# Computing the last group's slot shares ahead of the first expert layer

## The chip, the cores and the metric

The kernel runs on one core of a Trainium2 chip. The metric is the time of one execution on the device, in microseconds (us). All arithmetic is float32. TensorE (PE in the profile) multiplies and transposes; its weight loads are listed apart as PEld. VectorE (DVE), ScalarE (ACT) and GpSimd (POOL) do the element-wise work, and SyncE (SP) issues nearly all transfers between main memory and the core.

## The reference

Two blocks run one after the other. The first is a causal attention with exponential decay, without softmax, worked in blocks of the sequence with a carried state; its output is the input x (3072 rows of 512) of the second, a mixture of experts with soft routing: 8 experts of 4 slots each.

```python
logits = x @ phi                                  # 3072 x 32
d = exp(logits - logits.max(0)); d /= d.sum(0) + 1e-9     # over the rows, for each slot
slot_input = (d.T @ x).reshape(8, 4, 512)
for e in range(8):
    h = maximum(slot_input[e] @ w1[e], 0)         # 512 -> 1024, first layer
    slot_out[e] = h @ w2[e]                       # 1024 -> 512, second layer
c = exp(logits - logits.max(1)); c /= c.sum(1) + 1e-9     # over the slots, for each row
y = c @ slot_out
```

The shares c are needed only in the last line. They depend on the logits alone, so that they can be computed anywhere between the logits and the output.

## The kernel before, in words

The 3072 rows are cut into 24 tiles of 128 rows, two of which make a unit of the attention loop (line 483), and four make a group of the routing. For each of the six groups, `logits` (line 362) computes the logits with the slots on the partitions, keeps a running maximum and sum for d, and leaves a raw copy in `L`; `slot_softmax` (line 406) computes that group's shares c from the logits turned to rows on the partitions (`lp`), and writes them to `CN`. It is a generator with three stops: DVE takes a maximum (`cmx`) and subtracts it (`ce`), ACT takes the exponential; DVE sums (`cs`), adds 1e-9 and inverts; POOL multiplies into `CN`. Inside the loop a group's shares are computed in the unit after its logits. The last group has no unit after it, so its `lp` is made behind the loop: PE turns `L` into the PSUM bank `tr` (line 615).

Then come the experts. Their 4 + 4 split makes two units, Q = 0 and Q = 1. `first(Q, between)` (line 656) multiplies the slot inputs with w1 into two PSUM banks, one for each half of the 1024 hidden columns: `gl` and `xb` for Q = 0, `xa` and `tr` for Q = 1. So the second unit of the first layer writes over the bank in which `lp` lies. Its matmuls go in four steps of 128 input columns (kc), and in each step first to one bank (four matmuls), then to the other. After them ACT (bank 0) and DVE (bank 1) apply the scale and the ReLU into `h`, and DVE turns `h` in two pieces into `hz`, the weights of the second layer. In the first unit, `denominators` (line 644) runs between kc = 1 and kc = 2: it makes the second half of the slot inputs (`e`, turned by DVE, which kc = 2 and 3 read) and the scale `rown`.

`second(part, dst, fill)` (line 694) is the second layer. It makes the output's columns in two halves: `kv` for the first, `xa` for the second. In each half the blocks of Q = 0 come before those of Q = 1. During the second half the outputs of the first are already made (`spread`, `put`), and those of the second half follow at the end. The last group's `CN` is first read in `last_C` (line 768), during the second half.

Every engine works its instructions in the order in which this program text issues them (`InOrder`, line 38), and each waits where it reads or overwrites what another engine has not finished. The instructions below line 713 are therefore in this order on each engine.

Weights of w1 lie in 32 buffers of the pool `slabs`, all loaded long before the first layer. As the first unit gives these buffers back, the 16 remaining pairs of w2 tiles (`w2p`, 512 KB each) are loaded into them by the loop of line 714, and later `h`, `hz`, the spread sums and the outputs `o` take buffers of the same pool, in the order in which buffers become free.

Of the kernel before, what the change touches and what calls it, by code (L numbers as in the profile page):

```python
# [23 lines left out]
G = T // 4  # L24
# [29 lines left out]
def decay_attn_soft_moe(  # L54
# [23 lines left out]
    def bank(tag):  # L78
        return ps.tile([P, 512], F32, tag=tag, name=tag)
# [35 lines left out]
    def load_two(pool_=slabs, tag="slab", bufs=None):  # L115

        (Q, f, q), _ = late.pop(), late.pop()
        t_ = pool_.tile([P, 2, 512], F32, tag=tag, name="w2p", bufs=bufs)
        sp.dma_start(out=t_, in_=w2[4 * Q + q:4 * Q + q + 2, f].rearrange("e p d -> p e d"))
        for i in range(2):  # L120
            wt["w2", Q, q + i, f] = t_[:, i, :]
# [39 lines left out]
    for hh in range(2):  # L161
        for hp in range(HP):
            x = hh * HP + hp
# [242 lines left out]
    def slot_softmax(g, lp):  # L406

        lv = lp.rearrange("p (g s) -> p g s", g=4)
        cmx = small.tile([P, 4], F32, tag="cmx", name="cmx")
        dve.tensor_reduce(out=cmx, in_=lv, axis=AX.X, op=ALU.max)  # L410
        ce = small.tile([P, 4, SL], F32, tag="ce", name="ce", bufs=1)
        dve.tensor_tensor(
            out=ce, in0=lv, in1=cmx.rearrange("p (g o) -> p g o", o=1).broadcast_to([P, 4, SL]), op=ALU.subtract
        )
        act.activation(out=ce, in_=ce, func=AF.Exp)
        cs = small.tile([P, 4], F32, tag="cs", name="cs")
        yield
        dve.tensor_reduce(out=cs, in_=ce, axis=AX.X, op=ALU.add)
        dve.tensor_scalar(out=cs, in0=cs, scalar1=1e-9, scalar2=None, op0=ALU.add)
        dve.reciprocal(out=cs, in_=cs)  # L420
        yield
        pool.tensor_tensor(
            out=CN[:, 4 * g:4 * g + 4, :],
            in0=ce,
            in1=cs.rearrange("p (g o) -> p g o", o=1).broadcast_to([P, 4, SL]),
            op=ALU.mult,
        )
        yield
# [185 lines left out]
    lp = bank("tr")[:, 0:P]  # L614
# [41 lines left out]
    def first(Q, between=None):  # L656
        ph = [bank("gl"), bank("xb")] if Q == 0 else [bank("xa"), bank("tr")]
        for kc in range(4):
            for nf in range(2):
                for q in range(4):  # L660
                    pe.matmul(
                        out=ph[nf][SL * q:SL * q + SL, :],
                        lhsT=sT[:, kc, :],
                        rhs=wt["w1", Q, q, kc][:, nf, :],
                        start=(kc == 0),
                        stop=(kc == 3),
                    )
            if between is not None and kc == 1:
                between()
        if Q == 1:  # L670
            hz.append(slabs.tile([P, 32, SL], F32, tag="slab", name="hz"))
        h = slabs.tile([P, 2, 512], F32, tag="slab", name="h")
        act.activation(out=h[:, 0], in_=ph[0], func=AF.Relu, scale=rown[:, Q:Q + 1])
        dve.tensor_scalar(out=h[:, 1], in0=ph[1], scalar1=rown[:, Q:Q + 1], scalar2=0.0, op0=ALU.mult, op1=ALU.max)

        for nf in range(2):
            dve.transpose(
                out=hz[Q][:, 16 * nf:16 * nf + 16].rearrange("p a b -> p (a b)"), in_=h[:, nf]
            )
# [3 lines left out]
    def quad(dst, Q, f, w, start, stop):  # L683
        for q in range(4):
            pe.matmul(
                out=dst[SL * q:SL * q + SL],
                lhsT=hz[Q][:, 4 * f + q],
                rhs=w(q),
                start=start,
                stop=stop,  # L690
                skip_group_check=True,
            )

    def second(part, dst, fill):
# [13 lines left out]
        for n, (d_, Q, f, w) in enumerate(todo):  # L708
            if n in fill:
                fill[n]()  # L710
            quad(d_, Q, f, w, n == 0, n == len(todo) - 1)

    first(0, denominators)
    while late:
        load_two()
    for x in slot_softmax(G - 1, lp):
        pass
    first(1)

    so = work.tile([P, D], F32, tag="at", name="so", bufs=4)  # L720
# [119 lines left out]
```

## Time and profile before

| | us |
|---|---|
| median of 3 runs | 162.25 (162.06 to 162.30) |
| the profiled execution | 162.07 |
| its span, from the first to the last instruction | 160.3 |
| PE busy in it | 145.9 |
| DVE, ACT, POOL busy | 81.3, 49.4, 48.4 |

The span is 1.77 us shorter than the time of the same execution: what lies before the first and behind the last instruction. In the rows below, one matmul of the program is up to two records, since a float32 product is recorded in parts: a row with x8 is four matmuls of the first layer. Every instruction of the program carries line 48, where a helper issues it, so that rows are told apart by the names of the tiles. Names are printed without buffer numbers (`sc` is `sc0` or `sc1`, `s` is `s4`).

### The profile page before, as it was taken

To read this page: it belongs to the slowest core of one execution; us is meant where nothing else is said; L and a number is where in the kernel's file an instruction comes from. 1 tells how busy PE (TensorE), PEld (TensorE's weight loads), DVE (VectorE), ACT (ScalarE), POOL (GpSimd) and SP (SyncE) were. 2 spreads that over 40 slices of the span, in tenths; PEclk is the share of its full clock that TensorE was granted. 3 is DMA by queue.
4 is the path that set the end of the run, shared out by engine and by line. 5 is a ranking of instruction groups with operands and counts; after the bars stand their busy time and mean duration, and the time that the engine had idled before them with its cause. 6 is when DMAs were issued, how large, how long until landed. Compare 5 with 4: busy or idle time off the path is not lost.

```text
span 160.3 us, 5707 instructions
## 1 busy us (share of the span) xinstructions
PE 145.9 (91%) x2403; PEld 111.3 (69%) x2403; DVE 81.3 (51%) x184; ACT 49.4 (31%) x113; POOL 48.4 (30%) x63
## 2 busy tenths in 40 slices
PE   7899999999999999999999999999959999996900
PEld 7779998789879997998979897874212464652600
DVE  1996447383767287727754755543151311622720
ACT  3112433334431445061516151442010101621610
POOL 1288923642923083732282552000000000000000
PEclk9999999999999999999999999999999999999975
DMA  5999999999999999999999996999999999799497
GB/s 166 328 394 400 413 405 408 408 408 412 410 406 411 410 415 404 414 400 385 404 407 404 404 327 189 354 360 374 405 404 408 408 404 403 271 315 335 152 384 255
DMA packets 30745, 59.16 MB, mean 369 GB/s; under 512 B 2944, under 2 KB 9216, under 8 KB 30720
## 3 DMA queue, kind: packets, MB, share of 16 engines
q1 hardware_dynamic: 30576, 58.80, 97.0%
q8 instruction: 19, 0.31, 0.8%
q14 instruction: 6, 0.05, 0.1%
q10 hardware_dynamic: 144, 0.01, 0.1%
HBM read 52.50 MB, written 6.29 MB: 367 GB/s over the span
## 4 chain that ended last, share of the span: by engine, by line
PE 85%; DVE 5%; DMA 2%; ACT 1%; issue 1%; DVEq 1%
PE xa L48 20%; PE sc L48 17%; PE tr L48 12%; PE gl L48 12%; PE kv L48 10%; PE xb L48 10%; PE dp L48 3%; DMA lam_sb<-lam_x 2%; DVE mask L48 2%; DVE qpow L48 1%; DVE hz L48 1%; ACT o L48 1%; DVEq L836 1%; DVE h L48 0%; DVE so L48 0%
## 5 line engine op out<-in xcount | busy, mean ns | idle before, releaser
L48 POOL TENSOR_TENSOR qs<-ld,qpow 128x512 f32<-128x512 f32 x20 | 25.3, 1276 | 11.0 <-PE xb L48 6.0
L48 ACT COPY x<-sc 128x512 f32<-128x512 f32 x22 | 11.8, 589 | 33.5 <-PE sc L48 33.5
L48 DVE TENSOR_TENSOR at<-sc,mask 128x512 f32<-128x512 f32 x24 | 15.4, 684 | 9.1 <-PE sc L48 9.1
L48 POOL TENSOR_TENSOR dec<-st,qpow 128x256 f32<-128x256 f32 x16 | 9.9, 621 | 26.8 <-DVE st L48 26.8
L48 PEld LDWEIGHTS sc<-ld 64*128 64x128 f32 x192 | 11.6, 187 | 5.5 <-issue 5.4
L48 PE MATMUL sc<-ld 64*128 64x128 f32 x192 | 13.9, 285 | 0.0
L48 PE MATMUL tr<-ld 64*128 64x128 f32 x96 | 12.7, 273 | 0.7 <-DMA ld<-kT 0.7
L48 DVE TENSOR_TENSOR st<-dec,kv 128x256 f32<-128x256 f32 x16 | 6.6, 413 | 13.1 <-PE kv L48 12.9
L48 PE MATMUL xa<-at,ld 128*64 128x128 f32 x192 | 13.1, 279 | 0.0
L48 PE MATMUL dp<-ld 64*128 64x128 f32 x96 | 12.7, 273 | 0.0
L48 PE MATMUL xb<-at,ld 128*64 128x128 f32 x192 | 12.5, 273 | 0.0
L48 PEld LDWEIGHTS tr<-ld 64*128 64x128 f32 x96 | 11.6, 188 | 0.9 <-DMA ld<-qT 0.9
L48 PE MATMUL sc<-ident,xt 128*128 128x128 f32 x88 | 12.0, 280 | 0.0
L48 PEld LDWEIGHTS dp<-ld 64*128 64x128 f32 x96 | 11.6, 188 | 0.0
L48 PEld LDWEIGHTS xa<-at,ld 128*64 128x64 f32 x192 | 10.2, 136 | 2.0 <-issue 1.8
L48 PE MATMUL xa<-qs,st 64*64 64x128 f32 x160 | 11.4, 277 | 0.0
L48 PE MATMUL xb<-qs,st 64*64 64x128 f32 x160 | 11.4, 277 | 0.0
L48 POOL TENSOR_TENSOR vd<-ld,mask 128x512 f32<-128x512 f32 x9 | 9.6, 1061 | 5.1 <-DVE mask L48 5.1
L48 PEld LDWEIGHTS sc<-ident,xt 128*128 128x128 f32 x88 | 9.4, 141 | 1.9 <-issue 1.4
L48 PEld LDWEIGHTS xb<-at,ld 128*64 128x64 f32 x192 | 10.6, 137 | 0.0
L48 DVE TENSOR_TENSOR kn<-dp,mask 128x512 f32<-128x512 f32 x10 | 6.9, 691 | 6.8 <-PE dp L48 6.8
L48 PEld LDWEIGHTS xa<-qs,st 64*64 64x64 f32 x160 | 8.5, 132 | 1.5 <-issue 0.2
(162 smaller groups left out, 283.2 us busy)
## 6 DMA issues: line engine op xcount, KB each, us to landing
slab<-w_x SPq DMA_DIRECT2D x32, 512.0 KB, 7.0
w2p<-w_x SPq DMA_DIRECT2D x18, 512.0 KB, 9.9
w2t<-w_x SPq DMA_DIRECT2D x28, 256.0 KB, 5.5
ld<-kT SPq DMA_DIRECT2D x24, 256.0 KB, 6.9
ld<-qT SPq DMA_DIRECT2D x24, 256.0 KB, 6.6
ld<-vN SPq DMA_DIRECT2D x24, 256.0 KB, 6.9
y<-o SPq DMA_DIRECT2D x24, 256.0 KB, 3.5
L<-phi_x SPq DMA_DIRECT2D x1, 64.0 KB, 4.4
```

The source lines that it names most:

```text
L48: return self._tc.keep_in_program_order(f(*args, **kwargs))
L836: with tile.TileContext(nc) as tc:
```

## The change

The two lines that run the last group's `slot_softmax` stand ahead of `first(0, denominators)` in place of behind it and behind the loads of w2. Nothing else is edited.

```diff
+    for x in slot_softmax(G - 1, lp):
+        pass
     first(0, denominators)
     while late:
         load_two()
-    for x in slot_softmax(G - 1, lp):
-        pass
     first(1)
```

On DVE, before, from the product `wl` (the last instruction ahead of the first layer) to the inverse of the sum `cs`; `e`, `rden` and `rown` belong to `denominators`, `h` and `hz` to the end of the first unit:

```order
L48 TENSOR_TENSOR wl<-wgt,lsum 128x1
L48 STREAM_TRANSPOSE e<-dp 128x32 x2
L48 TENSOR_SCALAR rden<-sc_2097 128x1
L48 RECIPROCAL rden<-rden 128x1
L48 TENSOR_TENSOR rown<-own_125,rden 128x2
L48 TENSOR_SCALAR h<-xb,rown 128x512
L48 STREAM_TRANSPOSE hz<-h 128x512 x2
L48 TENSOR_REDUCE cmx<-tr 128x4
L48 TENSOR_TENSOR ce<-tr,cmx 128x128
L48 TENSOR_REDUCE cs<-ce 128x4
L48 TENSOR_SCALAR cs<-cs 128x4
L48 RECIPROCAL cs<-cs 128x4
```

And in the changed kernel, from the same product to the same transposes:

```order
L48 TENSOR_TENSOR wl<-wgt,lsum 128x1
L48 TENSOR_REDUCE cmx<-tr 128x4
L48 TENSOR_TENSOR ce<-tr,cmx 128x128
L48 TENSOR_REDUCE cs<-ce 128x4
L48 TENSOR_SCALAR cs<-cs 128x4
L48 RECIPROCAL cs<-cs 128x4
L48 STREAM_TRANSPOSE e<-dp 128x32 x2
L48 TENSOR_SCALAR rden<-sc_2107 128x1
L48 RECIPROCAL rden<-rden 128x1
L48 TENSOR_TENSOR rown<-own_125,rden 128x2
L48 TENSOR_SCALAR h<-xb,rown 128x512
L48 STREAM_TRANSPOSE hz<-h 128x512 x2
```

Five instructions have gone ahead of seven others. On ACT the exponential of `ce` stands ahead of the first unit's `h` in the same way; POOL's order is unchanged.

On PE the order is unchanged, but not what is waited for. These are the first matmuls of `first(1)`, with the semaphores that they wait for in brackets; lines with - are of before, with + of the change:

```order
 L48 MATMUL xa<-slab,e 32x512 [waits Activation_49]
 L48 MATMUL xa<-slab,e 32x512 x3
-L48 MATMUL tr<-slab,e 32x512 [waits DVE_49]
-L48 MATMUL tr<-slab,e 32x512 x3
+L48 MATMUL tr<-slab,e 32x512 x4
 L48 MATMUL xa<-slab,e 32x512 x3
```

The first matmul into `tr` no longer carries a wait of its own for DVE.

On SP the order is unchanged too, but buffers of the pool are given out in another order. These are the last loads of w2 and the first output:

```order
 L48 DMA w2p<-w_x 128x2x512 [waits DMAHW5_49,PE_49]
 L48 DMA w2p<-w_x 128x2x512 [waits DMAHW6_49,PE_49]
-L48 DMA w2p<-w_x 128x2x512 [waits DMAHW7_49,DVE_49,Activation_49]
+L48 DMA w2p<-w_x 128x2x512 [waits DMAHW7_49,PE_49]
 L48 DMA y<-o 128x2x256 [waits DMAHW0_49,Activation_49]
```

The sixteenth load went into the buffer of the first unit's `h`; now it goes into that of the first w1 tile of the second unit, and `h`, `hz` and the first spread sum behind it each take the next buffer.

## Rows read from the trace of the kernel before

**Rows 1.** The page: busy time, share of the span and instructions of each engine

```profile
PE 145.9 (91%) x2403; PEld 111.3 (69%) x2403; DVE 81.3 (51%) x184; ACT 49.4 (31%) x113; POOL 48.4 (30%) x63
```

**Rows 2.** The page: the queue of SP's transfers: packets, MB, share of 16 engines

```profile
q1 hardware_dynamic: 30576, 58.80, 97.0%
```

**Rows 3.** The page: the chain that ended last, by engine

```profile
PE 85%; DVE 5%; DMA 2%; ACT 1%; issue 1%; DVEq 1%
```

**Rows 4.** That chain in order of time: start us, us, what

```profile
117.83 0.75 DVE h L48
118.58 1.21 DVE hz L48 x2
119.79 0.19 DVE cmx L48
...
120.07 0.30 DVE ce L48
120.37 0.04 issue
120.41 1.06 PE tr L48 x8
...
126.63 6.95 PE kv L48 x128
```

**Rows 5.** Timeline of PE, first layer: start, us, what [idle before, releaser]

```profile
116.64 1.04 PE L48 MATMUL xb<-slab,e 128*32 128x512 f32 x8
117.50 1.04 PE L48 MATMUL xa<-slab,e 128*32 128x512 f32 x8
120.41 1.06 PE L48 MATMUL tr<-slab,e 128*32 128x512 f32 x8 [1.88 <-DVE ce L48]
121.30 1.04 PE L48 MATMUL xa<-slab,e 128*32 128x512 f32 x8
```

**Rows 6.** Timeline of DVE over the same stage

```profile
110.07 0.16 DVE L48 TENSOR_TENSOR wl<-wgt,lsum 128x1 f32<-128x1 f32 x1
113.77 0.31 DVE L48 STREAM_TRANSPOSE e<-dp 128x32 f32<-128x32 f32 x2 [3.54 <-PE sc L48]
...
119.71 0.25 DVE L48 TENSOR_REDUCE cmx<-tr 128x4 f32<-128x128 f32 x1
...
121.26 0.18 DVE L48 RECIPROCAL cs<-cs 128x4 f32<-128x4 f32 x1
...
127.36 1.29 DVE L48 STREAM_TRANSPOSE hz<-h 128x512 f32<-128x512 f32 x2
```

**Rows 7.** Timeline of ACT over the same stage

```profile
108.48 0.59 ACT L48 COPY CN<-xa 128x512 f32<-128x512 f32 x1
116.89 0.69 ACT L48 ACTIVATE h<-gl,rown 128x512 f32<-128x512 f32 x1 [7.83 <-PE gl L48]
120.39 0.31 ACT L48 ACTIVATE ce<-ce 128x128 f32<-128x128 f32 x1 [2.81 <-DVE ce L48]
```

**Rows 8.** Tile w2p: loads and use; ns min/median/max, first and last start us

```profile
L48 PE MATMUL xa<-w2p,hz x128: 379/379/404, 133.4 to 145.6; 128*32 128x256 f32 x128
L48 SPq DMA_DIRECT2D w2p<-w_x x18: 367/384/822, 108.3 to 128.5; - x18
...
DMA to landing us min/median/max: 6.0/9.9/10.8
```

**Rows 9.** Stretches: us, busy of PE, PEld, DVE, ACT, POOL, PEclk, DMA share, GB/s

```profile
144.00:148.00 4.00, 2.58 (x45) 1.07 (x37) 1.14 (x3) 0.83 (x3) 0.00 (x0) 1.00 1.04 360
148.00:150.50 2.50, 2.23 (x33) 1.76 (x36) 1.29 (x2) 1.07 (x2) 0.00 (x0) 1.00 0.03 11
150.50:159.00 8.50, 1.85 (x22) 1.02 (x16) 2.58 (x4) 2.15 (x4) 0.00 (x0) 0.73 1.05 370
```

**Rows 10.** Timeline of POOL: the last group's shares

```profile
121.59 0.40 POOL L48 TENSOR_TENSOR CN<-ce,cs 128x128 f32<-128x128 f32 x1 [12.70 <-DVE cs L48]
```

## The prediction

> **What bounds the kernel now.** I read four views, from the coarse to the fine. The page's busy times first [rows 1]: PE is busy 91% of the span, the other engines half of it or less, so what the change does to DVE, ACT or POOL matters only where PE waits for them. Then the transfers [rows 2]: the queue is busy 97% of the span, which makes it a second candidate for the bound. Third the chain of waits [rows 3]: 85% of it is PE, 5% DVE and 2% transfers. On average, then, PE sets the end; but the change sits in one stage, and there the answer has to be read.
>
> In that stage the chain leaves PE once [rows 4]. It runs over DVE: the first unit's `h` at 117.83, its two transposes to 119.79, then `cmx` and `ce` of the last group's shares to 120.37, and back to PE at 120.41. The timeline of PE shows the hole [rows 5]: the second unit's first matmuls into `xa` start at 117.50, the next ones, into `tr`, at 120.41, with 1.88 us idle put down to DVE's `ce`. The reason is the bank: the turned logits lie in `tr`, DVE has not read them, and they stand on DVE's queue behind `h` and `hz`, which themselves need the end of the first unit. So PE waits for two small readings of a bank that was filled before the first layer began (line 615).
>
> **What the change removes.** In the new order `cmx` and `ce` follow `wl`, which ends at 110.07 + 0.16 = 110.23 [rows 6]. The bank is then read, and free, about 7 us before PE wants it, and the wait on `tr` goes. What is it worth? The idle time says 1.88 us. The starts say more: groups of eight records follow each other every 0.86 us (116.64 to 117.50 [rows 5]), so the `tr` group would have started at 117.50 + 0.86 = 118.36, and it started at 120.41: 2.05 us late. The group behind it came 121.30 - 120.41 = 0.89 us later where 0.86 is the rule, so the restart cost another 0.03 us. Together 2.08 us, which I take; the idle time, 1.88, is the lower bound, since it counts from the end of the last matmul as printed, and that overlaps the next start (1.04 us long, 0.86 us apart). More than 2.08 can't come from this wait, as the matmuls around it already run at their usual distance.
>
> The Trainium skill ("Perfetto Trace Analysis", section "Tensor Engine Instruction (MATMUL, LD_WEIGHTS)") says that a matmul's end in the trace is estimated from its size, not observed. The rows agree: groups of 1.04 us stand 0.86 us apart. By the printed ends the sum would be 1.88, by the starts 2.08.
>
> **What it adds in the new place.** Five DVE instructions, one on ACT, one on POOL, no transfer. On DVE the whole chain, with its stop for ACT, took from 119.71 to 121.26 + 0.18 = 121.44, that is 1.73 us [rows 6]. Begun at 110.23 it ends at about 112.0. The next work on DVE is the transposing of `e`, which began at 113.77 after 3.54 us of idleness, waiting for PE. The cover is this idleness, and 113.77 - 112.0 = 1.8 us of it are left. Behind the chain on DVE stand the `e` transposes, for which PE's kc = 2 matmuls wait; were the cover gone, each us past 113.77 would cost one. On ACT the exponential took 0.31 us [rows 7]; ACT is free from 108.48 + 0.59 = 109.07 to 116.89, where `h` waits for PE, so it costs nothing. POOL's 0.40 us [rows 10] come some 9 us earlier and nothing stands behind them. The bounds of the added work: nothing, and 1.73 us if the chain found no cover at all. I take nothing, because the cover is twice as long as the chain.
>
> **What is late next.** All behind the hole is moved 2.08 us forward; I look for what doesn't move along.
>
> First, the second layer. Its first half starts with the blocks of Q = 0, which read the `hz` ready at 119.79 [rows 4]; PE will arrive at about 126.63 - 2.08 = 124.6. After half of its 6.95 us it needs the second unit's `hz`: before, at 126.63 + 3.48 = 130.1, with that `hz` done at 127.36 + 1.29 = 128.65 [rows 4, 6]. Both hang on the second unit's matmuls and move together, so 1.4 us of slack stay.
>
> Second, the weights, which don't move, since their transfers are saturated. The last `w2p` was issued at 128.5 and landed at most 10.8 us later, at 139.3; the last matmul that reads them started at 145.6 [rows 8]. After the change that is 143.5, still 4 us behind. The sixteenth load's other buffer comes free with the second unit's first step, at about 119.2, far ahead of its issue at 128.5. I take nothing here.
>
> Third, the outputs. Those of the second half took 8.5 us at 370 GB/s from 150.5 on, after 2.5 us in which the transfers nearly stood still, at 11 GB/s [rows 9]. The first half is as much again. If it had to wait until 139.3 for the last weights, it would be out by 139.3 + 8.5 = 147.8, and the second half starts at 150.5 - 2.08 = 148.4. So even this pessimistic line leaves 0.6 us, and the end moves with PE.
>
> **The sum.** 162.07 - 2.08 = 160.0 for the profiled execution, whose time is 0.18 us under the median of 162.25. Against the median, which is what will be compared, 162.25 - 2.08 = 160.17, so 160.2.
>
> **Rivals.** *A: the outputs of the first half collide with the weights and then with those of the second half.* For it: the transfers are at 1.04 of their share until 148 before [rows 9], and the first outputs will now be ready about 2 us sooner, beside the last loads. Against it: the 2.5 us at 11 GB/s that follow, of which the change uses at most 2.08. It decides once the first half's transfers end past 148.4, so once they are more than 0.6 us longer than the 8.5 us that I gave them. With a stretch of 1.4 us in excess, 0.8 us is lost and the time is 161.0.
>
> *B: the transfers are the bound, and the hole on PE was free.* With the queue at 97% [rows 2], what PE gains would be handed back as a wait for weights in the second layer. It would take loads landing 2 us after their use; they land 6 us before it (139.3 against 145.6 [rows 8]). The time would be 162.2. That the wait on `tr` stays for some other reason ends at the same time: the bank's other users are long done by then, so I give it little.
>
> The Trainium skill ("Perfetto Trace Analysis", section "Identifying the Most-Contended Engine") would have one judge transfers by their use of memory bandwidth and work on the most contended engine first. By that rule, with the queue at 97%, a wait on PE is worth nothing here. The trace disagrees for the stages behind the change: the transfers stand nearly still for 2.5 us shortly before the last outputs, waiting for PE's results.
>
> *C: the moved chain holds up DVE, slower than before.* The place is kc = 2 of the first unit: PE waited there for the `e` transposes at 113.77, and the chain with its round over ACT now stands ahead of them. It costs nothing until the chain lasts longer than 1.73 + 1.8 = 3.5 us, and outweighs the gain only past 3.5 + 2.08 = 5.6 us, over three times what it took. At 6.2 us the time would be 162.25 + 0.6 = 162.9. For it speaks only that DVE must wait for ACT in its middle; against it, that ACT is idle for 7.8 us there [rows 7].
>
> **How the numbers follow.** The forecast 0.87, A 0.07, B 0.04, C 0.02. The likeliest case's own range is 162.06 - 2.08 = 160.0 to 162.30 - 1.88 = 160.4, and a little for what the medians of a few runs differ by: 159.9 to 160.5. The range goes to A's end: 159.8 to 161.0. A measurement of this kernel tells a change of over 0.2% (0.3 us) from none, as its runs lie within 0.24 us. Faster are the forecast and A, 0.94; no change B, 0.04; slower C, 0.02.
>
> **What would show it.** In the profile after, the first group into `tr` of the second unit starts 0.86 us behind that into `xa`, at about 118.4, with no idle time before it. On DVE `cmx` starts at about 110.3 and the chain ends at about 112.0, with the `e` transposes still at about 113.8 and still released by PE. ACT's exponential is near 111. The second layer starts near 124.5, PE's last output matmuls come 2.1 us sooner, and the transfers still pause before the last outputs, with the span near 158.2. I am wrong if PE waits for a transfer in the second layer, if the pause is gone and the last outputs queue up, or if the `e` transposes come later than 113.8.

## The result, and the profile after

The changed kernel takes 160.06 us (159.98 to 160.25, 4 runs) against 162.20 us (162.06 to 162.30), a ratio of 0.9872 with a 95% interval from 0.9859 to 0.9884. It is faster by 2.14 us; 2.08 were forecast.

The profiled execution of it took 160.25 us, the longest of its four, with a span of 158.5 us. Its timeline of PE at the place of [rows 5]:

```profile
116.86 1.04 PE L48 MATMUL xb<-slab,e 128*32 128x512 f32 x8
117.72 1.04 PE L48 MATMUL xa<-slab,e 128*32 128x512 f32 x8
118.57 1.04 PE L48 MATMUL tr<-slab,e 128*32 128x512 f32 x8
119.43 1.04 PE L48 MATMUL xa<-slab,e 128*32 128x512 f32 x8
```

The group into `tr` now follows the one into `xa` after 0.85 us, with no idle time in brackets, and the next one after 0.86. All three distances are the usual ones: the wait is gone, and so is the slow restart behind it.

DVE and ACT over the same stage, as in [rows 6, 7]:

```profile
110.29 0.16 DVE L48 TENSOR_TENSOR wl<-wgt,lsum 128x1 f32<-128x1 f32 x1
110.37 0.28 DVE L48 TENSOR_REDUCE cmx<-tr 128x4 f32<-128x128 f32 x1
110.76 0.29 DVE L48 TENSOR_TENSOR ce<-tr,cmx 128x128 f32<-128x128 f32 x1
111.42 0.28 DVE L48 TENSOR_REDUCE cs<-ce 128x4 f32<-128x128 f32 x1 [0.38 <-ACT ce L48]
...
111.95 0.18 DVE L48 RECIPROCAL cs<-cs 128x4 f32<-128x4 f32 x1
113.99 0.31 DVE L48 STREAM_TRANSPOSE e<-dp 128x32 f32<-128x32 f32 x2 [1.86 <-PE sc L48]
...
125.50 1.30 DVE L48 STREAM_TRANSPOSE hz<-h 128x512 f32<-128x512 f32 x2
```

```profile
111.08 0.31 ACT L48 ACTIVATE ce<-ce 128x128 f32<-128x128 f32 x1 [1.80 <-DVE ce L48]
117.11 0.69 ACT L48 ACTIVATE h<-gl,rown 128x512 f32<-128x512 f32 x1 [5.72 <-PE gl L48]
```

The chain ends at 112.13, and DVE is still idle for 1.86 us ahead of the transposes of `e`, which are still released by PE. Before it was idle for 3.54; the chain took 1.68 of it.

The chain that ended last, by engine, as in [rows 3]; and the loads and stretches of [rows 8, 9], the stretches 2 us earlier:

```profile
PE 92%; ACT 1%; DVE 1%; issue 1%; DVEq 1%; ACTq 0%
```

```profile
L48 PE MATMUL xa<-w2p,hz x128: 379/379/403, 131.5 to 143.7; 128*32 128x256 f32 x128
L48 SPq DMA_DIRECT2D w2p<-w_x x18: 367/405/840, 108.0 to 128.9; - x18
...
DMA to landing us min/median/max: 6.3/10.1/10.7
```

```profile
146.00:148.50 2.50, 2.05 (x30) 1.59 (x32) 1.24 (x3) 1.07 (x2) 0.00 (x0) 1.00 0.08 27
148.50:157.00 8.50, 2.03 (x25) 1.20 (x18) 2.75 (x5) 2.15 (x4) 0.00 (x0) 0.81 1.03 364
```

The loads did not come earlier (last issue 128.9, before 128.5), their last use did, by 1.9 us. The pause ahead of the second half's outputs is still there, at 27 GB/s in place of 11.

Why the span of this execution is only 1.82 us shorter: everything up to `wl`, which is the same program in both, was 0.22 us later in it (110.29 against 110.07). From `wl` on, PE's start of the second layer moved from 126.44 to 124.58, which is 1.86 against the clock of the span and 2.08 against `wl`. This is its row before, and then after, with ACT's `h` of the second unit:

```profile
126.44 0.83 PE L48 MATMUL kv<-w2t,hz 128*32 128x256 f32 x12
```

```profile
124.58 2.77 PE L48 MATMUL kv<-w2t,hz 128*32 128x256 f32 x48
```

```profile
124.05 0.69 ACT L48 ACTIVATE h<-xa,rown 128x512 f32<-128x512 f32 x1 [6.26 <-PE xa L48]
```

A last 0.04 us went lost at the first output, where ACT's copy moved by 1.82 (137.21 to 135.39) and DVE's beside it by 1.86 (137.25 to 135.39). In the new order of buffers this copy takes that of the first unit's `h` and waits for one engine more. In all seven kernels in which it takes that buffer it starts within 0.01 us of DVE's copy; in the two in which it doesn't (before, and the one below with half of the second unit) it starts 0.04 us sooner. The buffer alone wasn't tried.

So executions are best compared from `wl` to the issue of the last output, as long as the outputs don't queue up behind that issue. In each profiled execution, us:

| | start of wl | last output issued | between | against before |
|---|---|---|---|---|
| before | 110.07 | 156.14 | 46.07 | |
| changed | 110.29 | 154.32 | 44.03 | -2.04 |
| other bank | 110.06 | 154.11 | 44.05 | -2.02 |
| reads only | 110.39 | 154.43 | 44.04 | -2.03 |
| between h and hz | 110.04 | 154.98 | 44.94 | -1.13 |
| two chains | 110.18 | 154.22 | 44.04 | -2.03 |
| three chains | 110.16 | 156.11 | 45.95 | -0.12 |
| half of the second unit | 110.29 | 152.28 | 41.99 | -4.08 |
| one copy | 110.67 | 154.05 | 43.38 | -2.69 |

### The profile page after: what moved, and what is told of

The parts are those of the page before. It is cut to its first block, busy times and chain, and to the rows that moved or that the text cites. A ratio compares the mean times of both kernels' runs of the same rounds, so it can differ in the third digit from the quotient of the medians.

```text
span 158.5 us, 5708 instructions
## 1 busy us (share of the span) xinstructions
PE 146.8 (93%) x2403; PEld 112.6 (71%) x2403; DVE 81.4 (51%) x184; ACT 49.4 (31%) x113; POOL 48.4 (31%) x63
## 4 chain that ended last, share of the span: by engine, by line
PE 92%; ACT 1%; DVE 1%; issue 1%; DVEq 1%; ACTq 0%
PE xa L48 21%; PE sc L48 19%; PE tr L48 13%; PE gl L48 12%; PE kv L48 11%; PE xb L48 10%; PE dp L48 6%; ACT o L48 1%; DVEq L836 1%; DVE so L48 0%; ACT so L48 0%; DVE s L48 0%; ACT s L48 0%; ACT e L48 0%; DVE e L48 0%
## 5 line engine op out<-in xcount | busy, mean ns | idle before, releaser
L48 PEld LDWEIGHTS sc<-ld 64*128 64x128 f32 x192 | 12.5, 199 | 5.6 <-issue 5.6
L48 PE MATMUL sc<-ld 64*128 64x128 f32 x192 | 14.8, 297 | 0.0
```

Of the source, the lines that this page charges most:

```text
L48: return self._tc.keep_in_program_order(f(*args, **kwargs))
```

## The experiments

The theory: the whole gain is PE's wait for bank `tr`, and the moved chain is free as long as it fits into DVE's idle time ahead of the `e` transposes. Rivals: it is DVE's and ACT's work that mattered, or the buffers of the pool, which the new order gives out differently; and, for the size, that the transfers take some of it back.

**The wait removed another way.** The old order, with another bank for the second unit:

```diff
-        ph = [bank("gl"), bank("xb")] if Q == 0 else [bank("xa"), bank("tr")]
+        ph = [bank("gl"), bank("xb")] if Q == 0 else [bank("xa"), bank("sc1")]
```

> The kernel before, in its old order, but the second unit of the first layer writes into bank sc1 in place of tr, so that nothing of it waits for the reading of the turned logits. Theory (the whole gain is the wait on bank tr, 2.08 us): about 160.1 us, as fast as the changed kernel, though cmx and ce still stand behind hz on DVE; no idle time of PE between the xa group and the sc1 group. Rival (the gain comes from taking DVE and ACT work out of the stretch around the second unit, or from the other buffers that the new order gives out): about 162.2 us, or somewhere between.

Measured: 160.31 us (160.04 to 160.40), ratio 0.9883 [0.9866, 0.9899], and from `wl` on 0.02 us more than the changed kernel. The timelines of PE and, last, of DVE:

```profile
117.48 1.04 PE L48 MATMUL xa<-slab,e 128*32 128x512 f32 x8
118.34 1.04 PE L48 MATMUL sc<-slab,e 128*32 128x512 f32 x8
```

```profile
118.48 1.29 DVE L48 STREAM_TRANSPOSE hz<-h 128x512 f32<-128x512 f32 x2
119.70 0.25 DVE L48 TENSOR_REDUCE cmx<-tr 128x4 f32<-128x128 f32 x1
```

`cmx` stands where it stood before, at 119.70 (119.71 in [rows 6]), and PE doesn't wait. So the DVE work behind `hz` is harmless in itself; what cost the time was that PE needed its bank. The buffers are not told apart by this run: its program, though in the old order, gives them out as the changed kernel's does.

**A part of the change alone.** Only the first stage ahead:

```diff
+    shares = slot_softmax(G - 1, lp)
+    next(shares)
     first(0, denominators)
...
-    for x in slot_softmax(G - 1, lp):
+    for x in shares:
         pass
```

> Only the first stage of the shares (cmx, ce and the exponential) stands ahead of the first layer; the sum, its inverse and the product stay where they stood before. Theory: the two readings of bank tr carry all of the gain, so about 160.1 us, the same as the changed kernel within 0.2. Rival (the late sum, inverse and product matter too): between 160.3 and 162.2 us.

Measured: 160.34 us (160.09 to 160.63), ratio 0.9883 [0.9867, 0.9899]; from `wl` on the same as the changed kernel to 0.01 us. The median lies 0.28 us over the changed kernel's, more than the 0.2 that the theory allowed and within the rival's range. The two intervals overlap, and since nothing is lost behind `wl`, the late sum, inverse and product are not what the 0.28 comes from; what it comes from isn't shown. In its timeline of DVE the sum is back behind `hz`:

```profile
110.86 0.29 DVE L48 TENSOR_TENSOR ce<-tr,cmx 128x128 f32<-128x128 f32 x1
...
118.82 1.29 DVE L48 STREAM_TRANSPOSE hz<-h 128x512 f32<-128x512 f32 x2
120.04 0.24 DVE L48 TENSOR_REDUCE cs<-ce 128x4 f32<-128x128 f32 x1
```

Two of the chain's five DVE instructions carry the gain.

**A place in the middle.** The chain between the first unit's `h` and its transposes:

```diff
-    first(0, denominators)
+    first(0, denominators, lambda: [x for x in slot_softmax(G - 1, lp)])
...
+        if behind_h is not None:
+            behind_h()
         for nf in range(2):
             dve.transpose(
```

> The whole chain stands between the first unit's h and its transposes hz on DVE. cmx should start about 0.05 us behind the end of h (118.58 in the trace of before), ce end some 0.65 us later, and the group into tr start near 119.25 in place of 118.36: 0.9 us late. Theory: the time follows the start of that group one to one, so about 161.0 us, about 1.2 below before. Rival (the place doesn't matter as long as hz isn't ahead of it, or hz late by 1.7 us holds up the second layer): 160.1 or above 161.5 us.

Measured: 161.14 us (160.94 to 161.23), ratio 0.9930 [0.9916, 0.9945]. DVE's `ce` and PE's wait for it:

```profile
118.85 0.29 DVE L48 TENSOR_TENSOR ce<-tr,cmx 128x128 f32<-128x128 f32 x1
```

```profile
117.47 1.04 PE L48 MATMUL xa<-slab,e 128*32 128x512 f32 x8
119.20 1.07 PE L48 MATMUL tr<-slab,e 128*32 128x512 f32 x8 [0.69 <-DVE ce L48]
```

The group into `tr` starts 1.73 us behind the one into `xa`, 0.87 more than the usual 0.86, and the time from `wl` on lies 0.91 over the changed kernel's: one to one, with the restart. The idle time in brackets, 0.69, would have said less, as 1.88 did before. This kernel, like all that were tried but the one with half of the second unit, has the changed kernel's buffers, so no run takes the wait and the buffers apart. The trace does: the first work in the changed kernel that uses a buffer given out differently is ACT's `h` at 124.05, the sixteenth load comes at 128.9, and by PE's start of the second layer at 124.58, which waits for neither, the whole 2.08 us are won.

**More than fits.** The chain is worked two and three times ahead of the first layer:

```diff
-    for x in slot_softmax(G - 1, lp):
-        pass
+    for _ in range(3):
+        for x in slot_softmax(G - 1, lp):
+            pass
     first(0, denominators)
```

> The changed kernel with the chain worked twice ahead of the first layer (the same values again). The second pass ends near 114.05 in the changed kernel's trace, where the e transposes started at 113.99, so they move by about 0.1 us. Theory (the cover is the idle time of DVE ahead of the e transposes, and what is inside it costs nothing): 160.1 to 160.3 us, as the changed kernel, though DVE does 1.7 us more work there. Rival (each chain costs its time): about 161.1 us, half of what the three cost.

> The changed kernel with the chain worked three times ahead of the first layer (the same values again). Each further pass waits for POOL's product of the one before, so about 2.0 us each: the third ends near 116.1 in the changed kernel's trace, and the e transposes start 2.1 us later than 113.99. Theory (rival C of the prediction with its threshold): the gain is eaten up, about 162.2 us, with PE waiting about 2.5 us for e ahead of kc = 2. Rival (the cover is larger than the idle time of DVE says, since PE has other work there): 160.1 to 161 us.

Measured: two 160.11 us (160.06 to 160.19), ratio 0.9866 [0.9850, 0.9883]; three a median of 162.24 us (161.90 to 163.89), ratio 1.0023 [0.9991, 1.0054], which is not told from before. Three of its ten runs took 163.6 us or more; why isn't shown. First two chains, then three, each DVE and then PE:

```profile
113.80 0.18 DVE L48 RECIPROCAL cs<-cs 128x4 f32<-128x4 f32 x1
113.89 0.30 DVE L48 STREAM_TRANSPOSE e<-dp 128x32 f32<-128x32 f32 x2
```

```profile
114.15 1.06 PE L48 MATMUL gl<-slab,e 128*32 128x512 f32 x8 [0.36 <-DVE e L48]
```

```profile
115.72 0.18 DVE L48 RECIPROCAL cs<-cs 128x4 f32<-128x4 f32 x1
115.81 0.28 DVE L48 STREAM_TRANSPOSE e<-dp 128x32 f32<-128x32 f32 x2
```

```profile
116.06 1.07 PE L48 MATMUL gl<-slab,e 128*32 128x512 f32 x8 [2.28 <-DVE e L48]
```

With two, DVE's idle time is used to the end, the `e` transposes follow at once, and PE waits for them as long as before, 0.36 us. With three it waits 1.92 us more (2.28), and 0.12 us of the gain are left from `wl` on. All buffers are again those of the changed kernel.

**How much further.** Half of the second unit's product is left out, to move PE's work behind it forward:

```diff
-        for kc in range(4):
+        steps = (4, 2)[Q]
+        for kc in range(steps):
```

> The changed kernel with the second unit of the first layer cut to two of its four steps of input columns: it leaves out half of that unit's product, to move all PE work behind it forward by another 4 x 0.86 = 3.43 us. What is asked is how much of a further gain on PE the transfers would let through. In the changed kernel the last w2 load lands at 139.1, the first half's 12 outputs land without a break from 139.98 to 147.36, 0.67 us apart, and the second half's first lands at 150.17, where an unbroken row would have it at 148.03: 2.14 us of slack. Theory (as the prediction put it, the end is PE's until the outputs follow the loads without a break): the gain is about 2.1 of the 3.43 us, about 157.9 us, and the pause between the outputs is gone. Rival A or B (the change had already used the slack up): 160.0 us. Rival (transfers bind nowhere): 156.6 us.

Measured: 158.87 us, between 158.22 and 159.72, ratio 0.9794 [0.9758, 0.9829]: 1.2 us under the changed kernel, where the theory had 2.1 and PE's work 3.43. That is a miss by one us. Its stretches around the outputs:

```profile
146.00:148.00 2.00, 1.05 (x10) 0.61 (x10) 1.90 (x4) 1.44 (x3) 0.00 (x0) 1.00 0.78 267
148.00:155.50 7.50, 0.00 (x0) 0.00 (x0) 0.01 (x1) 0.00 (x0) 0.00 (x0) 0.62 1.02 359
```

The kind of limit is as expected: the pause is nearly gone, and PE has no work left after 148. In this trace the outputs of the second half land from 148.66 on, 0.94 us behind those of the first, and the last at 156.05; in the changed kernel the last lands at 157.64. Both executions reach `wl` at 110.29, so 1.59 us came through in this one, and not the 2.14 expected. (The table's row stops at the last issue and would say 2.04; from that issue to its landing it was 3.77 us here and 3.32 there.) The pause between the halves shrank by 1.87 us, from 2.81 to 0.94, but the last load landed 0.36 us later, at 139.46 against 139.10, and the outputs follow it. Over the nine profiled executions this landing lies between 138.74 and 139.81. Where the outputs follow the loads without a break, such a difference would reach the end; whether that is why the runs of this kernel spread over 1.5 us, where the changed kernel's lie within 0.27, stays open.

**A version beyond both.** The small results are moved by one instruction:

```diff
-        n = HD // 2
-        act.copy(out=out_[:, 0:n], in_=in_[:, 0:n])
-        dve.tensor_copy(out=out_[:, n:HD], in_=in_[:, n:HD])
+        act.copy(out=out_[:, 0:HD], in_=in_[:, 0:HD])
```

> The changed kernel, and the small results of the second layer (so) and their spread copies (s4) are moved from PSUM by one ACT instruction for all 256 columns, in place of ACT and then DVE for 128 each, which wait for each other: 0.27 + 0.29 us and a handover (144.19 to 144.78). The same move of 128x256 took ACT 0.37 us elsewhere (CN<-xb). PE waits for three of the four pairs, so 3 x 0.22 = 0.66 us less if the gain still reaches the end. Theory (the end still follows PE after the change): 159.4 us. Rival B (the transfers bind): 160.1 us.

Measured: 159.44 us (159.40 to 159.97), ratio 0.9833 [0.9816, 0.9851], 0.62 us under the changed kernel; 0.65 from `wl` on. One pair in the changed kernel (ACT, then DVE), and its successor:

```profile
144.19 0.27 ACT L48 COPY so<-xa 128x128 f32<-128x128 f32 x1 [1.70 <-PE xa L48]
```

```profile
144.48 0.29 DVE L48 COPY so<-xa 128x128 f32<-128x128 f32 x1 [1.74 <-ACT so L48]
```

```profile
144.35 0.37 ACT L48 COPY so<-xa 128x256 f32<-128x256 f32 x1 [1.70 <-PE xa L48]
```

0.37 us in place of 0.58 for the pair, three times on the path. The end still follows PE, so after the change the transfers had not yet become the bound.

## Why the prediction was right

What bounds: the rows that mattered were the chain's and PE's [rows 4, 5], and the other-bank kernel shows that the link read from them, `hz` to `cmx` to `ce` to `tr`, was the cause.

The worth of the wait: 2.08 was taken from the starts and 1.88 from the idle time as a lower bound. Against `wl` PE's second layer moved by 2.08, and the kernel between `h` and `hz` repeated the difference at another size (0.69 idle, 0.87 late, 0.91 in time). The Trainium skill says in "Perfetto Trace Analysis", section "Tensor Engine Instruction (MATMUL, LD_WEIGHTS)", that the ends of matmuls are estimated; both traces agree, in that the printed ends overlap the next starts.

The chain in its new place: its cost, taken as nothing, was right. It began at 110.37, 0.08 us before the printed end of `wl` (110.29 + 0.16 = 110.45), where my line began it at that end, and took 1.76 us where 1.73 were taken over. The `e` transposes came at 113.99, and later than 113.8 had been named as a sign of being wrong; but they stand 3.70 us behind `wl` in both executions, so only the opening was later. Rival C had its place and its threshold right as well: no cost at two chains (3.6 us), all but 0.12 us of the gain gone at three (5.6 us), where the prediction had put the point of balance.

What is late next: the second unit's `hz` (125.50 + 1.30 = 126.80) came before PE's need of it, which moved with it; no matmul waited for a weight, the last load landing 4.2 us before its first use; the first half's outputs ended before the second half's. Here a size was wrong, on the careful side. I gave 0.6 us of slack on the line through the last load, and the trace of the changed kernel shows 2.1 us: its first half landed without a break from 139.98 to 147.36, and the second half's first output at 150.17, 2.14 us later than an unbroken row would have it. My line set the landing of the first half's last output against the start of the second half's first. Taken so, the trace gives 0.63 us as well (147.36 against an issue at 147.99):

```profile
147.99 6.89 SPq L48 DMA_DIRECT2D y<-o  x12
```

But this is not the room that the transfers have: the last of the first half is told as landed at 147.36, while hardly anything moves from 146.0 on (27 GB/s in the stretches above). With half of the second unit 1.87 us of it could be used. Nor did the change itself use up the pause, as rival A feared. Between the landings of the two halves there were 2.51 us before (149.49 to 152.00) and 2.81 after, since the first half moved forward too, by 2.12 us (142.10 to 139.98). Its first output now lands 0.88 us behind the last load, where it was 2.95 before, so that a further gain comes mostly out of the pause.

Rivals A and B did not occur. B's rule, as the prediction drew it from the Trainium skill ("Perfetto Trace Analysis", section "Identifying the Most-Contended Engine"), gave the transfers the first place at 97%. That figure is the queue's busy time, where the section asks for the memory bandwidth used, so the rule was not quite applied as it stands. The runs decide here: the one-copy kernel and the changed one both gained on PE alone, and only the half-unit kernel, 3.4 us further on, met them.

## What to carry to other kernels

When the busiest engine waits, look at what stands ahead of its releaser on the releaser's queue: a short reading of a shared bank queued behind long work holds the bank until that work is done. Here moving it into an earlier idle stretch and giving the waiting engine another bank were worth the same. Price a hole on PE by the starts of its matmuls against their usual distance, not by the idle time printed. Price the new place by the idle time ahead of what it will now precede: here all of 3.5 us could be filled for nothing, and in the one kernel that went well past it, by 1.92 us, the gain fell by as much.

## What the runs showed of the hardware

The same opening of the program took up to 0.63 us more in one profiled execution than in another (`wl` started between 110.04 and 110.67 in nine of them), which is more than some effects measured here; a mark behind the opening removes it. And two engines that moved a PSUM result of 128x256 in turn took 0.58 us from start to end (0.27 on ACT, then 0.29 on DVE), where ACT alone took 0.37.
